# Decode through two layers: cache tiles of 8 MB in two places, fixed places for the weights

## The chip, the cores and the metric

The kernel runs on one core of a Trainium2 chip. The metric is the time of one execution on the device in microseconds (us), the median of several runs. The core has a matrix engine (PE, with its weight loads shown as PEld), a vector engine (DVE), a scalar engine (ACT), GpSimd (POOL), and a sync engine (SP) that here issues nearly all loads. Sixteen DMA engines move the data between main memory and the on-chip buffer, whose 128 partitions hold all tiles.

## What is computed

One decode step of a small transformer, for 8 sequences of one token each, through an attention block and an MLP, and then once more through the same two blocks with the same weights and the same caches. All data are float32.

```
x = A_x                                        # (8, 1, 1024)
repeat twice:
    h = layernorm(x)
    q = (h @ wq) -> 8 x 32 heads x 128         # wq 1024 x 4096
    scores = q . k_cache * 128**-0.5           # caches 8 x 4 heads x 4096 x 128
    o = softmax(scores) . v_cache              # 8 query heads share a cache head
    x = x + o @ wo                             # wo 4096 x 1024
    h = layernorm(x)
    x = x + gelu(h @ w1 + b1) @ w2 + b2        # w1 1024 x 3584, w2 3584 x 1024
```

Keys and values are 8 MB each for one sequence ("batch" below), 128 MB in all, and are read in both layers. wq and wo have 16 MB each, w1 and w2 14 MB each.

## The kernel before

**One stream of loads.** All caches and weights are cut into tiles, and `stream` lists them in the order in which they are wanted. They go into one arena of 52 units of 0.5 MB (1024 float32 columns in each partition). `pump` (L207) takes the first tile of the stream, looks among the starting units that its entry allows for a run of free units (`Arena.take`, L57: the run that has been free longest, then the lowest), issues its DMA on SP and goes on; if there is no free run it returns. `release` (L219) frees a tile's units once the matmuls that read it have been written into the program, and pumps again. So the order of DMAs on SP is fixed when the program is built, each DMA waits on the chip until the last reader of the bytes that it overwrites is done, and a DMA that waits holds up all behind it. The waits follow the bytes, not the tiles: a load over half an old tile waits for that half's readers alone.

**Layer 0.** wq's first half (`q0`, unit 0, 8 MB) goes to units 0 to 15 and stays there for layer 1 (`kept`, as eight parts). wq's second half goes to 32 to 47. Its last 2048 columns ahead of the last `KEEP` ones are copied to PSUM, and the last `KEEP` to `spare` (`park`, L466), so that layer 1 needn't load them again. The caches of batches 0 to 7 go through units 16 to 47 in tiles of 4 MB, four places (`KV_AT`); only the last values have two tiles of 2 MB (`HALF_AT`). Units 48 to 51 are for the scores and the probabilities (`OWN`). The keys of the last batch stay in 16 to 31, since layer 1 takes the batches in reverse order. The weights wo, w1 and w2 then run through units 32 to 51 in tiles of mostly 2 MB, at any start that is a multiple of the tile (`ring`); the rows of w2 are taken second half first, and the first half is kept for layer 1 in units 32 to 45 (L522). Then follows what layer 1 needs of wq's second half: three tiles of 1 MB at 46, 48, 50 and three at 0, 2, 4, where `q0`'s kept parts lie until layer 1 has multiplied them.

**Layer 1.** The caches use units 0 to 31 in four places of 4 MB; wo, w1 and the second half of w2 then run through the same units in tiles of 4, 3, 2, 1 and 0.5 MB (`deep`).

**Attention for one batch** (`plan`, L426): eight key pieces of 1 MB, each four matmuls of 32 x 512 columns (`scores`, L350); the scaled copy with its maximum on DVE (L355), `probs` (exp on ACT, L371), `turn` (transposes, L381), and eight value pieces (`values`, L400), two for each of the four cache heads. After each cache head DVE sums four strips (L403, L405), `heads` multiplies them by a selector on PE (L412) and DVE scales the result (L413).

**Products with weights.** `expand` (L234) makes q and the hidden layer in two units u = 0, 1 of columns; when a unit is done its row is scaled on DVE, and its finishing step (`query_unit`, or `hidden_unit` with bias and gelu) is put in `pending`, to be written by the next `flush`, after the next tile's matmuls. `project` (L301) multiplies by wo and w2, one "kt" of 128 rows at a time: four matmuls of 256 columns, each counted twice in the profile (as are all float32 matmuls), so 8 passes for a kt. The bias b2 enters through `add_b2` after 16 kt. In layer 1, w2's kept half (14 kt, six tiles) comes first, then the streamed half.

Every load but the small first one (x and biases, on ACT) is issued by L214; the result is stored by L550.

Of the kernel before, what the change touches and what calls it, by code (L numbers as in the profile page):

```python
# [8 lines left out]
F32 = mybir.dt.float32  # L9
# [17 lines left out]
T = CH // P  # L27
NR = NH * HKV
# [6 lines left out]
SCW = W // 2  # L35
N_UNIT = 52
OWN = 48
RING = 32
R_AT = (46, 48, 50)
KV_AT = (16, 24, 32, 40), (0, 8, 16, 24)  # L40
HALF_AT = (32, 36, 40, 44), ()
QW = 40
Q_AT = (0, (B + 1) * QW - 32, (B + 1) * QW - 8, 32)
KEEP = SCW + CH
DMA_SCRATCH = 1024


class Arena:
# [49 lines left out]
def decode_layers(ctx: ExitStack, tc: tile.TileContext, x, kc, vc, wq, wo, w1, w2, out):  # L98
# [6 lines left out]
    ps_o = ctx.enter_context(tc.tile_pool(name="ps_o", bufs=2, space=PSUM))  # L105
# [19 lines left out]
    x_row, b1T, b2T = xb[:, 0:Q4], xb[:, Q4:Q4 + NFT], xb[:, Q4 + NFT:]  # L125
# [3 lines left out]
    oT, xnT = oxT[:, 0:HQ * B + PAD], oxT[:, HQ * B:]  # L129
# [7 lines left out]
    hT = oT  # L137
# [20 lines left out]
    def flush():  # L158
        while pending:
            pending.pop(0)()  # L160
# [10 lines left out]
    def row_sums():  # L171
        return by_turns("r")
# [31 lines left out]
    stream = []  # L204
# [18 lines left out]
        slot.free()  # L223
        pump()

    def tiles(name):
        i = 0
        while (name, i) in held:
            yield held.pop((name, i))
            i += 1  # L230
        if (*name, "end") in held:
            yield held.pop((*name, "end"))

    def expand(name, unit, rs, finish, hooks={}, last=None):  # L234
        for u in range(2):
            acc = ps_o.tile([P, CH], F32, tag="o", name="acc")
            at = 0
            begun = set()
            end = NT * unit
            starts = [P * sum((unit // P - e + 3) // 4 for e in range(j)) for j in range(5)]  # L240
            for i, slot in enumerate(tiles((name, u))):
                c = 0
                while c < slot.cols and at < end:
                    kt, a = divmod(at, unit)
                    n = min(unit - a, slot.cols - c)
                    for j in range(4):
                        d0, d1 = max(a, starts[j]), min(a + n, starts[j + 1])
                        if d0 < d1:
                            nc.tensor.matmul(acc[32 * j:32 * j + 32, d0 - starts[j]:d1 - starts[j]],  # L249
                                             xnT[:, kt * B:kt * B + 32], slot.ap[:, c + d0 - a:c + d1 - a],  # L250
                                             start=(j not in begun), stop=(kt == NT - 1 and d1 == starts[j + 1]))
# [46 lines left out]
        if u == 1 and st["layer"] == 0:  # L298
            nc.gpsimd.memset(qz[:, 0:2 * nt * B], 0.0)

    def project(name, ks, lhs, out_row, resid, rsum, hooks={}):  # L301
        y = ps_o.tile([P, CH], F32, tag="o", name="y")
        n = 0
        for i, slot in enumerate(tiles(name)):
            for c in range(0, slot.cols, D):
                kt = ks[n]
                for j in range(4):
                    nc.tensor.matmul(y[32 * j:32 * j + 32, 0:Q4], lhs[:, kt * B:kt * B + 32],  # L308
                                     slot.ap[:, c + j * Q4:c + (j + 1) * Q4],
                                     start=(n == 0), stop=(n == len(ks) - 1))  # L310
                n += 1
                if n in hooks:
                    hooks[n]()
                if name[0] == "p" and n == 2 * NT:
                    add_b2(y)
                if n == NR:
                    flush()
            release(slot)
            flush()
        assert n == len(ks)  # L320
        nc.vector.scalar_tensor_tensor(out_row, y[:, 0:Q4], 1.0, resid, op0=ALU.mult, op1=ALU.add, accum_out=rsum)  # L321
# [169 lines left out]
    def caches(layer, order, skip, cuts):  # L491

        for b in order:
            for a, where, dram in (("k", k_at, kc), ("v", v_at, vc)):
                r = 0
                for m in cuts.get((a, b), (4, 4)):
                    lane = [(a, *where(b, e)) for e in range(r, r + m)]
                    if lane[0] not in skip:
                        for e, key in enumerate(lane):
                            pieces[layer, key] = ((layer, lane[0]), e)  # L500
                        yield ((layer, lane[0]), 2 * m, dram[b][:, r * W:(r + m) * W], (KV_AT if m == 4 else HALF_AT)[layer], ())
                    r += m

    rsum = row_sums()
# [1 line left out]

    kept = {("k", *k_at(B - 1, r)) for r in range(NR)}
    orders = [list(range(B)), list(range(B))[::-1]]
    ring = lambda k, i: range(RING, N_UNIT - k + 1, k)
    deep = lambda k, i: range(0, RING - k + 1, 8 if k > 4 else k)  # L510
    fixed = lambda *at: lambda k, i: (at[i],)
    last_q = [2] * 5 + [2.5]
    early = NFT // 2

    weights(("q0", 0), wq[0], [16], fixed(0), kept=lambda i: [(("q1", 0), e) for e in range(8)])
    weights(("q0", 1), wq[1], [16], fixed(RING))
    stream.extend(caches(0, orders[0], (), {("v", B - 1): (4, 2, 2)}))
    weights("o0", wo[0], [4] * 8, ring)
    for u in range(2):
        weights(("i0", u), w1[u], [4, 4, 4, 2], ring)  # L520
    weights("p0", w2[0], [4, 4, 4, 2], ring, early * D)
    weights("p0", w2[0], [4, 4, 2, 2, 1, 1], fixed(32, 36, 40, 42, 44, 45), 0, 4, lambda i: [("p1", i)])  # L522
    weights(("q1", 1), wq[1], last_q, fixed(*R_AT, 0, 2, 4))
    stream.extend(caches(1, orders[1], kept, {}))
    weights("o1", wo[0], [8] * 4, deep)
    for u in range(2):
        weights(("i1", u), w1[u], [8, 6], deep)
    weights("p1", w2[0], [4, 4, 2, 2, 1, 1], deep, early * D, 6)
    pump()
    for layer in range(2):  # L530
        st["layer"] = layer
        rs = layernorm(x_row, rsum)
        if layer == 0:
            expand("q0", W, rs, query_unit, last=park)
        else:
            held["q1", 1, "end"] = Kept(spare)
# [3 lines left out]
        project(f"o{layer}", range(HQ), oT, x_row, x_row, rsum, {4: last})  # L540
        rs = layernorm(x_row, rsum)
        expand(f"i{layer}", F // 2, rs, hidden_unit)
        rsum = row_sums()
        ks = list(range(NFT))
        if layer == 0:
            flush()
            ks = ks[early:] + ks[:early]
        project(f"p{layer}", ks, hT, x_row, x_row, rsum)

    nc.sync.dma_start(out=out, in_=x_row)  # L550

# [56 lines left out]
```

## Time and profile before

| | |
|---|---|
| median of 3 runs | 871.49 us (871.17 to 872.06) |
| the profiled execution | 872.42 us, span 870.6 us |
| TensorE clock granted, mean | 0.806 |
| bytes read from main memory | 368.46 MB |
| loads issued by L214 | 111 |

The span reaches from the first to the last instruction of the program; 1.8 us of the profiled execution lie around it. Times in windows and timelines are us from the span's start. In a timeline row stand start, duration, engine, line, operation, output<-inputs, shape and count, and in brackets the idle time of the engine ahead of the group and what ended it. A window row has start:end and length, the busy time of each engine with its instructions in brackets, and at its end the granted clock, the DMA engines' busy share and GB/s. The slices in the page are 1/40 of the span, 21.8 us.

### The profile page before, as it was taken

The page shows a single profiled execution, that of the slowest core. Times are in us where ns is not written, and L with a number is a line of the kernel's source. Part 1 is how long each engine was busy: PE and PEld are TensorE (multiplying, and loading weights), DVE is VectorE, ACT ScalarE, POOL GpSimd, SP SyncE. Part 2 cuts the span into 40 slices and gives each one's busy share as a digit, 9 for nine tenths or more (in the row PEclk, how much of TensorE's full clock was granted, in tenths as well). Part 3 has the DMA queues.
Part 4 walks back from the last instruction along what each step waited for, and adds up shares of the span by engine and source line. Part 5 has one row for each costly group of instructions (what it writes and reads, how often), then busy time and mean ns, then how long its engine had stood idle before and what let it go on. Part 6 is the DMA issues. An engine that isn't in the chain of part 4 may idle for free.

```text
span 870.6 us, 9005 instructions
## 1 busy us (share of the span) xinstructions
PE 554.2 (64%) x3988; PEld 191.5 (22%) x3988; DVE 182.6 (21%) x588; ACT 48.7 (6%) x76; POOL 1.7 (0%) x11
## 2 busy tenths in 40 slices
PE   0477566756756555756768767665667667565667
PEld 0122121221212122222223222121222212122324
DVE  0013131313223131300111232131313222130002
ACT  0010000000000000000001100000000000000000
POOL 0000000000000000000000000000000000000000
PEclk9887886788688878888779987678768778777889
DMA  9999999999999999999999999999999999999997
GB/s 391 434 434 433 432 434 428 425 434 431 427 431 431 433 434 425 388 429 430 424 409 411 436 431 431 434 433 432 429 431 428 432 431 428 431 433 430 429 425 291
DMA packets 16312, 369.17 MB, mean 424 GB/s; under 512 B 1809, under 2 KB 2065, under 8 KB 2577
## 3 DMA queue, kind: packets, MB, share of 16 engines
q1 hardware_dynamic: 16128, 368.45, 98.9%
q8 instruction: 31, 0.51, 0.2%
q10 hardware_dynamic: 144, 0.15, 0.0%
q14 instruction: 9, 0.07, 0.0%
HBM read 368.46 MB, written 0.13 MB: 423 GB/s over the span
## 4 chain that ended last, share of the span: by engine, by line
DMA 75%; PE 20%; DVE 2%; issue 1%; ACT 1%; another core or an unknown queue 1%; SPq 0%; ACTq 0%; DVEq 0%
DMA arena<-in_k_dram 53%; PE sps L350 11%; DMA arena<-in_w_dram 10%; DMA arena<-in_wo_dram 7%; DMA arena<-in_wq_dram 6%; PE acc L249 3%; PE y L308 3%; PE o_ps L400 1%; PE sps L381 0%; PE sps L274 0%; DVE scr L405 0%; SPq L214 0%; ACT arena L371 0%; DVE arena L355 0%
## 5 line engine op out<-in xcount | busy, mean ns | idle before, releaser
L350 PE MATMUL sps<-arena,qz 128*32 128x512 f32 x1024 | 170.9, 827 | 103.4 <-DMA arena<-in_k_dram 102.1
L400 PE MATMUL o_ps<-arena 128*32 128x512 f32 x1024 | 156.1, 738 | 1.0 <-DMA arena<-in_v_dram 1.0
L308 PE MATMUL y<-arena,oxT 128*32 128x256 f32 x960 | 75.9, 469 | 42.0 <-DMA arena<-in_wo_dram 30.9
L350 PEld LDWEIGHTS sps<-arena,qz 128*32 128x32 f32 x1024 | 42.2, 145 | 228.9 <-issue 182.4
L249 PE MATMUL acc<-arena,oxT 128*32 128x512 f32 (+3 forms) x510 | 71.1, 652 | 31.9 <-DMA arena<-in_w_dram 20.8
L355 DVE TENSOR_SCALAR_CACHE_REDUCE arena<-sps 128x512 f32<-128x512 f32 x32 | 22.1, 692 | 238.2 <-PE sps L350 238.2
L405 DVE SCALAR_TENSOR_TENSOR scr<-o_ps,bits,scr 128x128 f32<-128x128 f32 x192 | 67.3, 351 | 6.8
L381 PE MATMUL sps<-ident,arena 128*128 128x128 f32 x128 | 29.8, 376 | 37.4 <-DVE oxT L413 22.7
L308 PEld LDWEIGHTS y<-arena,oxT 128*32 128x32 f32 x960 | 34.5, 131 | 81.0 <-DMA arena<-in_wo_dram 33.2
L371 ACT ACTIVATE arena<-arena,bits 128x1024 f32<-128x1024 f32 x16 | 18.4, 1147 | 538.1 <-DVE scr L368 507.1
L412 PE MATMUL sps<-bits,scr 128*128 128x8 f32 x128 | 25.1, 269 | 36.4 <-DVE scr L405 31.0
L400 PEld LDWEIGHTS o_ps<-arena 128*32 128x32 f32 x1024 | 31.6, 129 | 64.6 <-issue 59.8
L403 DVE TENSOR_SCALAR scr<-o_ps,bits 128x128 f32<-128x128 f32 x64 | 22.5, 351 | 92.8 <-PE o_ps L400 92.8
L412 PEld LDWEIGHTS sps<-bits,scr 128*128 128x128 f32 x128 | 19.3, 190 | 88.5 <-DVE scr L405 79.6
L249 PEld LDWEIGHTS acc<-arena,oxT 128*32 128x32 f32 x510 | 21.5, 121 | 71.9 <-issue 34.1
L381 PEld LDWEIGHTS sps<-ident,arena 128*128 128x128 f32 x128 | 19.2, 187 | 43.4 <-ACT arena L371 27.7
L364 PE MATMUL sps<-scr,bits 128*128 128x128 f32 x32 | 7.8, 326 | 21.3 <-DVE scr L360 21.3
L387 DVE COPY arena<-sps 128x512 f32<-128x512 f32 x16 | 11.1, 692 | 43.0 <-PE sps L381 43.0
L181 PE MATMUL sps<-ident,xb 128*128 128x128 f32 x16 | 4.0, 338 | 25.1 <-DMA xb<-in_x_dram 23.4
L321 DVE SCALAR_TENSOR_TENSOR xb<-y,xb 128x256 f32<-128x256 f32 x4 | 1.7, 425 | 81.3 <-PE y L308 81.3
L389 PE MATMUL sps<-scr,bits 128*128 128x32 f32 x32 | 10.2, 412 | 12.5 <-DVE arena L387 12.5
L413 DVE TENSOR_TENSOR oxT<-sps,scr 128x8 f32<-128x8 f32 x64 | 11.0, 171 | 29.8 <-PE sps L412 29.8
(67 smaller groups left out, 128.9 us busy)
## 6 DMA issues: line engine op xcount, KB each, us to landing
arena<-in_v_dram SPq DMA_DIRECT2D x31, 4096.0 KB, 29.0
arena<-in_k_dram SPq DMA_DIRECT2D x30, 4096.0 KB, 33.4
arena<-in_w_dram SPq DMA_DIRECT2D x13, 2048.0 KB, 20.0
arena<-in_wo_dram SPq DMA_DIRECT2D x8, 2048.0 KB, 16.4
arena<-in_wo_dram SPq DMA_DIRECT2D x4, 4096.0 KB, 33.3
arena<-in_w_dram SPq DMA_DIRECT2D x2, 4096.0 KB, 32.0
arena<-in_w_dram SPq DMA_DIRECT2D x7, 1024.0 KB, 21.2
arena<-in_w_dram SPq DMA_DIRECT2D x2, 3072.0 KB, 31.1
```

Source lines behind the costliest of these rows:

```text
L249: nc.tensor.matmul(acc[32 * j:32 * j + 32, d0 - starts[j]:d1 - starts[j]], xnT[:, kt * B:kt * B + 32], slot.ap[:, c + d0 - a:c + d1 - a], ...
L308: nc.tensor.matmul(y[32 * j:32 * j + 32, 0:Q4], lhs[:, kt * B:kt * B + 32], slot.ap[:, c + j * Q4:c + (j + 1) * Q4], start=(n == 0), stop= ...
L350: nc.tensor.matmul(ps[32 * g:32 * g + 32, :], qz[:, c:c + 32], kt[:, g * CH:(g + 1) * CH], start=(j == 0), stop=(j == HKV - 1))
L355: nc.vector.tensor_scalar(st["row", b].ap[:, half * CH:(half + 1) * CH], ps, SCALE, None, op0=ALU.mult, op1=ALU.max, accum_out=st["mx", b] ...
L371: nc.scalar.activation(row, row, AF.Exp, bias=bias, scale=1.0, accum_out=ls)
L381: nc.tensor.transpose(pp[:, t * P:(t + 1) * P], row[:, c:c + P], ident)
L387: nc.vector.tensor_copy(dst, src)
L400: nc.tensor.matmul(o[32 * g:32 * g + 32, :], s[:, g], v[:, g * CH:(g + 1) * CH], start=(half == 0), stop=(half == NH - 1))
L403: nc.vector.tensor_scalar(r, o[:, 0:P], sel_t[:, 0:1], None, op0=ALU.mult)
L405: nc.vector.scalar_tensor_tensor(r, o[:, t * P:(t + 1) * P], sel_t[:, t:t + 1], r, op0=ALU.mult, op1=ALU.add)
L412: nc.tensor.matmul(po[:, 0:REP], r_s[j % 2], sel_h, start=True, stop=True)
L413: nc.vector.tensor_tensor(oT_v[:, j * REP:(j + 1) * REP, b], po[:, 0:REP], rl_s[b % 2][:, j * REP:(j + 1) * REP], ALU.mult)
```

## The change

Caches now come in tiles of 8 MB, whole keys or values of a batch, in two places: units 16 and 32 in layer 0, 0 and 16 in layer 1 (`CACHE_AT`). `CUTS` names the few that are cut: the last batch of layer 0, the first two tiles that are loaded in layer 1, and its last values. The weights of layer 0 after the attention have tiles of 3 MB for the most part, each with a place given by hand (`fixed`); in layer 1 wo comes in two tiles of 8 MB. `KEEP` grows by 3 x 128 columns, `DMA_SCRATCH` falls from 1024 to 64, and the last tile of wq shrinks to match. `project` is split: `products` multiplies a number of tiles, and in layer 1 a hook in `expand` calls it after the second tile of w1's second half, for the first two kept tiles of w2 (12 kt, with b2 after 8); `project` then goes on from there.

```diff
-KV_AT = (16, 24, 32, 40), (0, 8, 16, 24)
-HALF_AT = (32, 36, 40, 44), ()
+CACHE_AT = (16, 48), (0, 32)
+CUTS = {(0, "k", B - 1): (4, 2, 2), (0, "v", B - 1): (2, 2, 2, 2), (1, "v", B - 1): (4, 4), (1, "k", B - 2): (4, 4), (1, "v", 0): (4, 4)}
-KEEP = SCW + CH
-DMA_SCRATCH = 1024
+KEEP = SCW + CH + 3 * P
+DMA_SCRATCH = 64
...
-    def project(name, ks, lhs, out_row, resid, rsum, hooks={}):
-        y = ps_o.tile([P, CH], F32, tag="o", name="y")
-        n = 0
-        for i, slot in enumerate(tiles(name)):
+    def products(y, name, ks, lhs, n, i0, m, hooks={}):
+        for i, slot in zip(range(m), tiles(name, i0)):
...
+    def project(name, ks, lhs, out_row, resid, rsum, hooks={}, begun=None):
+        y, n, i = begun or (ps_o.tile([P, CH], F32, tag="o", name="y"), 0, 0)
+        n = products(y, name, ks, lhs, n, i, len(ks), hooks)
...
-                for m in cuts.get((a, b), (4, 4)):
+                for m in CUTS.get((layer, a, b), (NR,)):
...
-                        yield ((layer, lane[0]), 2 * m, dram[b][:, r * W:(r + m) * W], (KV_AT if m == 4 else HALF_AT)[layer], ())
+                        at = range(CACHE_AT[layer][0], CACHE_AT[layer][1], 2 * m)
+                        yield ((layer, lane[0]), 2 * m, dram[b][:, r * W:(r + m) * W], at, ())
...
-    weights("o0", wo[0], [4] * 8, ring)
-    for u in range(2):
-        weights(("i0", u), w1[u], [4, 4, 4, 2], ring)
-    weights("p0", w2[0], [4, 4, 4, 2], ring, early * D)
-    weights("p0", w2[0], [4, 4, 2, 2, 1, 1], fixed(32, 36, 40, 42, 44, 45), 0, 4, lambda i: [("p1", i)])
+    weights("o0", wo[0], [4, 4, 6, 6, 6, 6], fixed(32, 36, 40, 46, 32, 40))
+    weights(("i0", 0), w1[0], [6, 6, 2], fixed(46, 32, 38))
+    weights(("i0", 1), w1[1], [6, 6, 2], fixed(40, 46, 38))
+    weights("p0", w2[0], [6, 6, 2], fixed(32, 40, 38), early * D)
+    weights("p0", w2[0], [6, 6, 1, 1], fixed(32, 40, 38, 39), 0, 3, lambda i: [("p1", i)])
...
-    weights("o1", wo[0], [8] * 4, deep)
-    for u in range(2):
-        weights(("i1", u), w1[u], [8, 6], deep)
-    weights("p1", w2[0], [4, 4, 2, 2, 1, 1], deep, early * D, 6)
+    weights("o1", wo[0], [16, 16], fixed(16, 0))
+    weights(("i1", 0), w1[0], [8, 6], fixed(16, 24))
+    weights(("i1", 1), w1[1], [4, 4, 4, 2], fixed(0, 4, 8, 12))
+    weights("p1", w2[0], [6, 4, 2, 1, 1], fixed(16, 24, 28, 22, 23), early * D, 4)
...
+            begun = []
+
+            def begin():
+                y = ps_o.tile([P, CH], F32, tag="o", name="y")
+                begun.extend((y, products(y, "p1", ks, hT, 0, 0, 2, {NT: add_b2}), 2))
+
+            expand("i1", F // 2, rs, hidden_unit, {(1, 1): begin})
+            rsum = row_sums()
+            project("p1", ks, hT, x_row, x_row, rsum, begun=begun)
```

More of the change, by code (lines that the diff above doesn't have):

```diff
@@ L224, in release, with tiles @@
         pump()
-    def tiles(name):
-        i = 0
+    def tiles(name, i=0):
         while (name, i) in held:
@@ L312, in project @@
                 if n in hooks:
-                    hooks[n]()
-                if name[0] == "p" and n == 2 * NT:
-                    add_b2(y)
+                    hooks[n](y)
                 if n == NR:
@@ L319, in project @@
             flush()
+        return n
+    def project(name, ks, lhs, out_row, resid, rsum, hooks={}, begun=None):
+        y, n, i = begun or (ps_o.tile([P, CH], F32, tag="o", name="y"), 0, 0)
+        n = products(y, name, ks, lhs, n, i, len(ks), hooks)
         assert n == len(ks)
@@ L489, in weights, with caches @@
             at += n
-    def caches(layer, order, skip, cuts):
+    def caches(layer, order, skip):
         for b in order:
@@ L508, in decode_layers, with fixed @@
     orders = [list(range(B)), list(range(B))[::-1]]
[L509 to L512, printed above, removed]
     early = NFT // 2
+    def fixed(*at):
+        return lambda k, i: (at[i],)
     weights(("q0", 0), wq[0], [16], fixed(0), kept=lambda i: [(("q1", 0), e) for e in range(8)])
     weights(("q0", 1), wq[1], [16], fixed(RING))
-    stream.extend(caches(0, orders[0], (), {("v", B - 1): (4, 2, 2)}))
-    weights("o0", wo[0], [4] * 8, ring)
-    for u in range(2):
-        weights(("i0", u), w1[u], [4, 4, 4, 2], ring)
-    weights("p0", w2[0], [4, 4, 4, 2], ring, early * D)
-    weights("p0", w2[0], [4, 4, 2, 2, 1, 1], fixed(32, 36, 40, 42, 44, 45), 0, 4, lambda i: [("p1", i)])
-    weights(("q1", 1), wq[1], last_q, fixed(*R_AT, 0, 2, 4))
-    stream.extend(caches(1, orders[1], kept, {}))
-    weights("o1", wo[0], [8] * 4, deep)
-    for u in range(2):
-        weights(("i1", u), w1[u], [8, 6], deep)
-    weights("p1", w2[0], [4, 4, 2, 2, 1, 1], deep, early * D, 6)
+    stream.extend(caches(0, orders[0], ()))
+    weights("o0", wo[0], [4, 4, 6, 6, 6, 6], fixed(32, 36, 40, 46, 32, 40))
[3 more added lines that the diff above has]
+    weights("p0", w2[0], [6, 6, 1, 1], fixed(32, 40, 38, 39), 0, 3, lambda i: [("p1", i)])
+    last_q = (2 * NR * SCW - W - KEEP) / SCW
+    last_q = [2] * 5 + [last_q - 10]
+    weights(("q1", 1), wq[1], last_q, fixed(*R_AT, 0, 2, 4))
+    stream.extend(caches(1, orders[1], kept))
+    weights("o1", wo[0], [16, 16], fixed(16, 0))
+    weights(("i1", 0), w1[0], [8, 6], fixed(16, 24))
+    weights(("i1", 1), w1[1], [4, 4, 4, 2], fixed(0, 4, 8, 12))
+    weights("p1", w2[0], [6, 4, 2, 1, 1], fixed(16, 24, 28, 22, 23), early * D, 4)
     pump()
@@ L539, in decode_layers @@
         rsum = row_sums()
-        project(f"o{layer}", range(HQ), oT, x_row, x_row, rsum, {4: last})
+        project(f"o{layer}", range(HQ), oT, x_row, x_row, rsum, {4: lambda y: last()})
         rs = layernorm(x_row, rsum)
-        expand(f"i{layer}", F // 2, rs, hidden_unit)
-        rsum = row_sums()
         ks = list(range(NFT))
         if layer == 0:
+            expand("i0", F // 2, rs, hidden_unit)
             flush()
-            ks = ks[early:] + ks[:early]
-        project(f"p{layer}", ks, hT, x_row, x_row, rsum)
+            rsum = row_sums()
+            project("p0", ks[early:] + ks[:early], hT, x_row, x_row, rsum, {2 * NT: add_b2})
+        else:
+            begun = []
[3 more added lines that the diff above has]
+            expand("i1", F // 2, rs, hidden_unit, {(1, 1): begin})
+            rsum = row_sums()
+            project("p1", ks, hT, x_row, x_row, rsum, begun=begun)
     nc.sync.dma_start(out=out, in_=x_row)
```

## The prediction

> **What bounds the kernel now.** I read the page first, then the windows, then the timelines of PE and SP.
>
> ```profile
> PE 554.2 (64%) x3988; PEld 191.5 (22%) x3988; DVE 182.6 (21%) x588; ACT 48.7 (6%) x76; POOL 1.7 (0%) x11
> GB/s 391 434 434 433 432 434 428 425 434 431 427 431 431 433 434 425 388 429 430 424 409 411 436 431 431 434 433 432 429 431 428 432 431 428 431 433 430 429 425 291
> q1 hardware_dynamic: 16128, 368.45, 98.9%
> q8 instruction: 31, 0.51, 0.2%
> DMA 75%; PE 20%; DVE 2%; issue 1%; ACT 1%; another core or an unknown queue 1%; SPq 0%; ACTq 0%; DVEq 0%
> ```
>
> One queue moves 368.45 MB, its packets fill 98.9% of the sixteen DMA engines' time, and no other engine is busy for more than 64%. In most slices the rate is 431 to 434 GB/s. At 434 the bytes alone are 368.45/0.434 = 849 us of the 870.6, so the change can win only bytes, overhead per DMA, or the 21.6 us that lie outside the full rate. These windows show where that is.
>
> ```profile
> 22.00:44.00 22.00, 10.16 (x92) 4.37 (x96) 1.87 (x5) 2.41 (x5) 0.00 (x0) 0.84 1.00 434
> 350.00:356.00 6.00, 5.73 (x33) 1.40 (x36) 1.93 (x6) 0.00 (x0) 0.00 (x0) 0.63 0.77 284
> 450.00:454.00 4.00, 1.13 (x16) 0.50 (x16) 0.00 (x0) 0.00 (x0) 0.00 (x0) 0.93 0.90 336
> 470.00:474.00 4.00, 4.00 (x48) 1.26 (x48) 0.16 (x1) 1.78 (x4) 0.00 (x0) 1.00 0.99 369
> 490.00:840.00 350.00, 224.26 (x1496) 76.84 (x1496) 80.07 (x261) 16.75 (x28) 0.00 (x0) 0.78 1.00 431
> 862.00:867.00 5.00, 5.00 (x98) 3.03 (x92) 0.00 (x0) 0.00 (x0) 0.00 (x0) 1.00 0.36 143
> ```
>
> The last two columns are the DMA engines' busy share and GB/s. Against 434 the hole at 350 costs 6 x 150/434 = 2.07 us, that at 450 costs 4 x 98/434 = 0.90, that at 470 costs 4 x 65/434 = 0.60. The last row says something else: 0.64 x 5 = 3.2 us of a mean engine are idle while the latest of the sixteen still works, so the engines drift some 3 us apart, and a tile has landed only when the latest has.
>
> **The steady batch.** These PE rows are one batch of layer 0: keys in two halves, values, next keys.
>
> ```profile
> 92.22 5.02 PE L350 MATMUL sps<-arena,qz 128*32 128x512 f32 x32 [3.33 <-DMA arena<-in_k_dram]
> 102.02 5.25 PE L350 MATMUL sps<-arena,qz 128*32 128x512 f32 x32 [4.77 <-DMA arena<-in_k_dram]
> 115.26 4.59 PE L400 MATMUL o_ps<-arena 128*32 128x512 f32 x24
> 126.89 1.07 PE L400 MATMUL o_ps<-arena 128*32 128x512 f32 x8
> 131.07 6.08 PE L350 MATMUL sps<-arena,qz 128*32 128x512 f32 x32 [3.11 <-DMA arena<-in_k_dram]
> out_dram<-xb SPq DMA_DIRECT2D x1, 128.0 KB, 1.7
> ```
>
> 131.07 - 92.22 = 38.85 us for four 4 MB tiles: 9.71 each. Half the keys take PE 5.0 to 6.1 us, from the end of the keys to the first value matmul 115.26 - 107.27 = 8.0 us pass (softmax and transposes), the values take 126.89 + 1.07 - 115.26 = 12.7 us. From issue to first byte I take 1.7 us, the whole of a 128 KB store, so an upper figure.
>
> With two places of 8 MB a place is reloaded only when all of it is read. Let the keys land at L. They are read by L + 10.6 (12.3 at worst, two halves of 6.1); the values land at L + 19.4 and start then, since L + 10.6 + 8.0 is earlier; they are read by L + 32.2. The keys' place can be filling at L + 10.6 + 1.7 = L + 12.3, needed at L + 19.4: **7 us spare**. The values' place can be filling at L + 33.9, and is needed when the next keys have landed, L + 38.7: **4.8 us spare** for the latest engine. The 3.2 us of drift fit in. So I cost the loss of four places at nothing; the cover is that 4.8 us.
>
> **The change, part by part.**
>
> *Bytes.* KEEP grows by 384 columns: 128 x 384 x 4 = 0.197 MB of wq are no longer read twice, 0.197/0.434 = **0.45 us**. The cost is a longer copy on ACT beside q0, ahead of the first value load, which is wanted only at 63; nothing. What the smaller DMA scratch does no row shows; every DMA on the page's list is issued by SP or ACT and keeps its form, so I put nothing.
>
> *Fewer DMAs.* Counting the stream in both files, 111 loads become 79: caches 63 to 39, wo 12 to 8, w1 12 to 12, w2 16 to 12, wq 8 in both. What one costs is read from tiles of other sizes.
>
> ```profile
> 376.94 1.93 PE L308 MATMUL y<-arena,oxT 128*32 128x256 f32 x32 [1.55 <-DMA arena<-in_wo_dram]
> 381.84 3.57 PE L308 MATMUL y<-arena,oxT 128*32 128x256 f32 x32 [2.96 <-DMA arena<-in_wo_dram]
> 465.41 0.64 PE L308 MATMUL y<-arena,oxT 128*32 128x256 f32 x8 [0.18 <-DMA arena<-in_w_dram]
> 466.68 0.64 PE L308 MATMUL y<-arena,oxT 128*32 128x256 f32 x8 [0.64 <-DMA arena<-in_w_dram]
> 1.18 42.44 DMA arena<-in_wq_dram
> ```
>
> 2 MB come every 4.90 us, 4 MB every 9.71, 0.5 MB every 1.27: two halves cost 2 x 4.90 - 9.71 = 0.09 us more than the whole. 8 MB at 434 GB/s are 19.33, against 2 x 9.71 = 19.42, again 0.09. The two 8 MB tiles of wq took 42.4 us together with start-up, the bias load and some code, and that is the bound from the bad side (rival C). Between 0 and 0.09 I take 0.06: 32 x 0.06 = **1.9 us**. The Trainium skill, DMA: Bandwidth & Descriptors, Anatomy of one DMA, fits 2.0 us of fixed cost for each DMA (fitted for DMAs from GpSimd, so its use for SP's queue is my stretch). In series that would be 64 us for 32 DMAs and no such sum fits these rows: here queued DMAs cover it (rival D).
>
> *The hole at 350.* The first wo tile goes where the first values of the last batch lay and is issued when head group 0 is read.
>
> ```profile
> 336.68 5.34 PE L350 MATMUL sps<-arena,qz 128*32 128x512 f32 x32 [4.35 <-DMA arena<-in_k_dram]
> 349.94 5.01 PE L400 MATMUL o_ps<-arena 128*32 128x512 f32 x24
> 353.64 22.15 SPq L214 DMA_DIRECT2D arena<-in_wo_dram  x8
> ```
>
> The last keys land at 336.5, so the values end at 336.5 + 9.7 + 4.9 + 4.9 = 356.0; wo can flow only from 353.64 + 1.7 = 355.3, and engines that are 3 us ahead stand idle. In the new kernel the last keys come in three pieces. The stream is 0.8 us earlier by then (13 joined pairs at 0.06), so the last piece lands at 335.9. Its 16 passes take 2.7 us, but the values of batch 6 end at 316.4 + 0.1 + 12.7 = 329.2, after which the three pieces run 5.4 + 2.7 + 2.7: keys read at 340.0, values from 348.0, head group 0 read at 351.7, wo flows from 353.4, while the values' last tile lands at 355.3. Engines over 1.9 us ahead still wait a little (about 0.35 in the mean). Gain 2.07 - 0.35 = **1.7 us**; bounds 0.6 (if the 1.3 us on the latest engine were code, see B) and 2.07.
>
> *The weights between.* Places of 3 MB are refilled when a tile 6 kt long is read, and each of wo, w1 has over 4 us spare: a 6-kt tile takes PE 4.5 us at most and 7.3 us to load, with two others ahead of it. The 450 hole came of four small tiles whose places waited for one tile; now the first kept w2 tile needs the first late tile (landing near 436, read by 440) and is wanted at 446. It goes: **0.9 us**; bounds 0 and 0.9.
>
> *A new wait at 470.* These rows show what ends w2 and starts q1.
>
> ```profile
> 445.75 4.48 PE L308 MATMUL y<-arena,oxT 128*32 128x256 f32 x48 [2.97 <-DMA arena<-in_w_dram]
> 469.35 1.07 PE L249 MATMUL acc<-arena,oxT 128*32 128x512 f32 x8
> 453.56 19.92 SPq L214 DMA_DIRECT2D arena<-in_wq_dram  x6
> 476.63 7.78 SPq L214 DMA_DIRECT2D arena<-in_v_dram  x2
> ```
>
> Three wq tiles (2.47 us each, 7.4 us) need no wait; the fourth waits for PE to read the first kept q1 tile (470.4 before, 3.8 us after the last w2 tile landed). Now the last 3 MB of w2 lands only 2.5 us ahead of the end, and its 6 kt take 4.5 us after a wait, then two single kt: PE finishes 2.8 us after the last landing instead of 0.7. So the fourth wq flows at 3.8 + 2.1 + 1.7 = 7.6 us after that landing and is needed at 7.4: 0.2 us for the latest engine, and those ahead lose their lead. Behind it on SP stand two wq tiles and all caches of layer 1. The first cache tile then waits for eight kept tiles as before, about 1 us ahead of need. Mean loss between 0.2 and 2, of which 0.6 was there: I take **-0.9 us**.
>
> *The end.* Multiplying the first 12 kept kt of w2 inside w1 moves 96 passes off the last stretch.
>
> ```profile
> 792.67 41.90 SPq L214 DMA_DIRECT2D arena<-in_w_dram  x10
> arena<-in_w_dram SPq DMA_DIRECT2D x1, 512.0 KB, 32.4
> 855.07 5.39 PE L308 MATMUL y<-arena,oxT 128*32 128x256 f32 x96
> 861.92 5.55 PE L308 MATMUL y<-arena,oxT 128*32 128x256 f32 x94
> 867.52 0.42 DVE L321 SCALAR_TENSOR_TENSOR xb<-y,xb 128x256 f32<-128x256 f32 x1 [5.91 <-PE y L308]
> ```
>
> The last tile is issued at 834.25 and lands 32.4 us later, 866.65; PE is done 0.87 later, against 0.7 after layer 0's last tile. In the new order 14 kt (6.3 us at 0.45) follow gelu, which ends about 8 us before the last landing: the tail stays, +0.1 to -1.0. I take **0**. The gain of that edit is that two 8 MB wo tiles, which let PE start w1 some 5 us later, cost nothing.
>
> **Sum.** 0.45 + 1.9 + 1.7 + 0.9 - 0.9 = 4.05 us. The profiled execution took 872.42 us, 1.8 around its span of 870.6; it becomes 868.4, and the median of the runs, 871.49, becomes **867.4**. Best ends: 0.45 + 2.9 + 2.07 + 0.9 + 0.4 + 0.1 = 6.8, so 864.7; one code load (0.51 MB/31 = 16 KB, 0.6 us on one engine) that misses the latest engine makes it 864.0. Worst: 0.45 + 0 + 0.6 + 0 - 1.4 - 1.0 = -1.35, so 872.8.
>
> **The rivals.**
>
> A, slower: the values' place comes free too late. Place: the 8 MB value load of every batch, behind L400. It decides from 4.8 us more on the chain keys, softmax, values; each us beyond is paid in each of about 12 batches with whole tiles. Against: the rows above. For: PE will stand idle 6 us at a stretch instead of 3 to 5, and a PE that has been idle is slower (granted clock 0.63 at 350, 0.58 in the window below; 1.00 in the last). Keys wholly at half speed would take 21 us, not 10.6: values start at L + 29, end at L + 41.7, 4.7 us late, x 12 = 56 us. Only part slow, 6 us on the chain: 1.2 x 12 = 14 us, 882 us. Chance 8%.
>
> ```profile
> 446.00:450.00 4.00, 4.00 (x48) 1.78 (x40) 0.00 (x0) 0.00 (x0) 0.00 (x0) 0.58 1.00 424
> ```
>
> The Trainium skill, TensorE: Matmul & The Clock Gate, HAM oscillation, speaks against the change here: gaps in PE work over about 3.4 us drop the clock to half. The rows agree in kind: 6.08 against 5.02 us for the same half after gaps.
>
> B, little gained: the change doesn't close the holes, because they are code loads, or the 470 wait takes what they gave. What stays is bytes and half of the overhead, 0.45 + 0.95 = 1.4 us: 870.1. For: the DMA share at 470 was 0.99 with only 369 GB/s, so not all of a hole is waiting. Chance 13%.
>
> C, slower: 8 MB tiles load worse, 20.5 us rather than 19.4 (42.44 less about 1.5 of start, halved). 28 such tiles more, 1.1 each: 31 us, 902 us. Against: 434 GB/s in the window 22 to 44, which moves nothing but wq. Chance 3%.
>
> D, 2 us saved for each DMA: 64 us, 807 us. Against: 368.1 MB in that time would be over 455 GB/s, and no slice has over 436. Chance 1%.
>
> **The numbers.** 0.2% is 1.7 us, about what a measurement of this kernel can tell from no change: faster is under 869.7, slower over 873.2. The forecast has 75%, nearly all of it faster; B 13%, three parts in four within 0.2%. Faster 0.75 + 0.01 + 0.01 = 0.77, same 0.11, slower 0.12. Range 864.0 to 872.0: the best end, and B with most of the worst end; A, C and D stay out.
>
> **What would show it.** Steady batches 0.1 to 0.3 us shorter than 38.85; value loads issued 4 to 5 us before the keys ahead of them land; 420 GB/s and more at 350 and 450; a hole at 470 of 1 to 2 us; last landing some 4 us earlier, then 0.7 to 1.0 us to the last DVE step. Slices under 425 GB/s all through the attention would make the prediction wrong by A or C: SP waiting for L400 beyond the landing is A, 20.5 us a tile without such a wait is C.

## The result and the profile after

The changed kernel takes **868.02 us** (median of 5 runs, 867.59 to 868.36) beside 872.06 us for the kernel before (871.17 to 873.39, 5 runs): ratio 0.9951, 95% interval 0.9936 to 0.9965. The profiled execution took 868.16 us with a span of 866.4 (before: 872.42 and 870.6). Run again beside the experiments it took 868.49 us (867.49 to 869.17), ratio 0.9953 (0.9941 to 0.9966).

From the page of the kernel after: totals, rate in slices of 21.7 us, the load queue, and the chain that ended last.

```profile
PE 526.5 (61%) x3998; PEld 188.6 (22%) x3998; DVE 182.6 (21%) x588; ACT 49.0 (6%) x76; POOL 1.7 (0%) x11
GB/s 393 437 436 433 436 430 433 433 433 433 436 434 433 436 405 430 430 429 428 428 404 404 440 444 433 430 430 433 433 436 433 436 433 430 415 446 430 412 428 294
q1 hardware_dynamic: 11520, 368.25, 99.0%
DMA 71%; PE 24%; DVE 3%; another core or an unknown queue 1%; issue 1%; ACT 0%; SPq 0%; ACTq 0%; DVEq 0%
```

The bytes are 0.20 MB fewer, the packets 4608 fewer. The slice at 350 (the 17th) has 430 GB/s where it had 388; the two slices from 433 to 477 have 404, so nothing was won there in the mean of the engines. The windows say the same (last columns: DMA share, GB/s). Slices and windows count a packet whole where it starts, and packets of an 8 MB tile have 64 KB and take 2.42 us, so a share can come out above 1.00 and a rate some per cent off: the 405 in the 15th slice is 431 when its packets are counted by the time that they lie in it.

```profile
350.00:356.00 6.00, 5.22 (x44) 1.61 (x36) 2.96 (x10) 0.00 (x0) 0.00 (x0) 0.88 1.01 431
446.00:450.00 4.00, 2.56 (x40) 1.14 (x32) 0.00 (x0) 0.00 (x0) 0.00 (x0) 0.87 0.98 410
450.00:454.00 4.00, 1.00 (x18) 0.64 (x20) 0.00 (x0) 0.00 (x0) 0.00 (x0) 0.98 0.98 356
454.00:460.00 6.00, 5.21 (x44) 1.84 (x38) 0.69 (x1) 0.00 (x0) 0.00 (x0) 0.50 0.92 390
466.00:470.00 4.00, 3.85 (x49) 1.19 (x52) 0.73 (x3) 2.06 (x4) 0.00 (x0) 1.00 0.97 383
490.00:840.00 350.00, 211.52 (x1518) 73.93 (x1514) 81.86 (x268) 18.34 (x30) 0.00 (x0) 0.79 1.00 432
```

The hole at 350 is closed (284 to 431). The one at 450 is still there, 356 GB/s, but at a share of 0.98: most engines are in packets that move less, and few are idle. In 490 to 840 the rate is 432 instead of 431.

The steady batch, from PE's timeline: both halves of the keys, the first and last value matmuls, and the next keys; then the value load in SP's timeline.

```profile
101.77 5.57 PE L350 MATMUL sps<-arena,qz 128*32 128x512 f32 x32 [7.00 <-DMA arena<-in_k_dram]
108.17 3.64 PE L350 MATMUL sps<-arena,qz 128*32 128x512 f32 x32 [0.83 <-DVE arena L355]
121.13 5.27 PE L400 MATMUL o_ps<-arena 128*32 128x512 f32 x24 [0.79 <-DMA arena<-in_v_dram]
132.75 1.07 PE L400 MATMUL o_ps<-arena 128*32 128x512 f32 x8
140.47 1.93 PE L350 MATMUL sps<-arena,qz 128*32 128x512 f32 x8 [6.66 <-DMA arena<-in_k_dram]
```

```profile
133.88 0.33 SPq L214 DMA_DIRECT2D arena<-in_v_dram  x1
```

A batch takes 140.47 - 101.77 = 38.70 us, where it took 38.85. PE takes 12.7 us for the values, as before, and 10.0 for the keys. The value load is issued at 133.88, 6.55 us ahead of the landing of the keys in front of it: less the 1.7 us to its first byte, 4.85 us are spare, as reckoned.

Where the 4.1 us arose is best seen in the landings of single loads (issue plus time to landing in the list of issues, us):

| landing of | before | after | gain so far |
|---|---|---|---|
| layer 0's last values | 356.03 | 355.23 | 0.80 |
| its last wo tile | 396.69 | 394.25 | 2.44 |
| its last w2 tile | 466.64 | 463.20 | 3.44 |
| the last wq tile | 482.11 | 479.51 | 2.60 |
| layer 1's last values | 776.08 | 771.36 | 4.72 |
| the last load | 866.64 | 862.52 | 4.12 |

### The profile page after: what moved, and what is told of

It reads as the page before. It is cut to its first block, busy times and chain, and to the rows that moved or that the text cites. A ratio compares the mean times of both kernels' runs of the same rounds, so it can differ in the third digit from the quotient of the medians.

```text
span 866.4 us, 8937 instructions
## 1 busy us (share of the span) xinstructions
PE 526.5 (61%) x3998; PEld 188.6 (22%) x3998; DVE 182.6 (21%) x588; ACT 49.0 (6%) x76; POOL 1.7 (0%) x11
## 4 chain that ended last, share of the span: by engine, by line
DMA 71%; PE 24%; DVE 3%; another core or an unknown queue 1%; issue 1%; ACT 0%; SPq 0%; ACTq 0%; DVEq 0%
DMA arena<-in_k_dram 47%; PE sps L350 16%; DMA arena<-in_w_dram 11%; DMA arena<-in_wo_dram 7%; DMA arena<-in_wq_dram 6%; PE y L305 3%; PE acc L248 2%; PE o_ps L400 2%; DVE arena L355 1%; DVE scr L405 1%; PE sps L381 0%; ACT arena L371 0%; PE sps L273 0%; PE sps L412 0%
## 5 line engine op out<-in xcount | busy, mean ns | idle before, releaser
L350 PE MATMUL sps<-arena,qz 128*32 128x512 f32 x1024 | 146.5, 721 | 109.2 <-DMA arena<-in_k_dram 96.8
L400 PE MATMUL o_ps<-arena 128*32 128x512 f32 x1024 | 154.3, 731 | 16.6 <-DMA arena<-in_v_dram 16.6
L350 PEld LDWEIGHTS sps<-arena,qz 128*32 128x32 f32 x1024 | 35.3, 129 | 216.9 <-issue 101.9
L248 PE MATMUL acc<-arena,oxT 128*32 128x512 f32 (+3 forms) x518 | 65.5, 607 | 25.4 <-DMA arena<-in_w_dram 14.2
L305 PEld LDWEIGHTS y<-arena,oxT 128*32 128x32 f32 x960 | 36.9, 134 | 86.9 <-issue 34.4
L381 PE MATMUL sps<-ident,arena 128*128 128x128 f32 x128 | 32.0, 397 | 37.5 <-DVE oxT L413 22.7
L248 PEld LDWEIGHTS acc<-arena,oxT 128*32 128x32 f32 x518 | 21.7, 117 | 60.2 <-issue 28.7
```

Source lines behind the costliest of these rows:

```text
L350: nc.tensor.matmul(ps[32 * g:32 * g + 32, :], qz[:, c:c + 32], kt[:, g * CH:(g + 1) * CH], start=(j == 0), stop=(j == HKV - 1))
L381: nc.tensor.transpose(pp[:, t * P:(t + 1) * P], row[:, c:c + P], ident)
L400: nc.tensor.matmul(o[32 * g:32 * g + 32, :], s[:, g], v[:, g * CH:(g + 1) * CH], start=(half == 0), stop=(half == NH - 1))
```

## The experiments

Times are medians; the changed kernel is at 868.0 (first five runs) and 868.5 (run again), the kernel before at 872.0 to 872.6.

**The changed kernel again.**

> The changed kernel beside the experiments. The sum's theory: bytes 0.45 us, 32 fewer DMAs 1.9, the hole at 350 1.7, the hole at 450 and the wait at 470 together 0, so about 4 us less than the kernel before, 868.0 again, with the last load landing near 862.5. A rival: the gain belongs to the pair of executions that were compared, and less than 2 us of it is left.

868.49 us, last load landing at 861.8. The gain is there again.

**Whole caches in 4 MB tiles.**

```diff
-                for m in CUTS.get((layer, a, b), (NR,)):
+                for m in CUTS.get((layer, a, b), (4, 4)):
```

> Only the tile size of the caches goes back: whole keys and values in two tiles of 4 MB each, places as they fall free, the small tiles at the last batch of layer 0 and all else as in the changed kernel. 105 loads instead of 79. Theory (0.06 us for each DMA): 26 x 0.06 = 1.6 us more than the changed kernel, 869.6, evenly along the attention, 38.85 us a batch instead of 38.7. Rival (the size of a tile costs nothing, the gain is in the holes alone): 868.0.

869.68 us (869.43 to 870.62), 1.2 to 1.7 more than the changed kernel, and evenly. Its PE timeline, the second key halves of two neighbouring batches:

```profile
102.23 5.34 PE L350 MATMUL sps<-arena,qz 128*32 128x512 f32 x32 [4.11 <-DMA arena<-in_k_dram]
141.09 2.79 PE L350 MATMUL sps<-arena,qz 128*32 128x512 f32 x12 [4.77 <-DMA arena<-in_k_dram]
```

141.09 - 102.23 = 38.86 us a batch instead of 38.70: 0.08 for each of two DMAs saved. By the landings it is 2 x 9.71 - 19.36 = 0.06. The theory holds.

**8 MB caches in the kernel before**, that is the same part from the other side.

```diff
-                for m in cuts.get((a, b), (4, 4)):
+                for m in CUTS.get((layer, a, b), (NR,)):
...
-KV_AT = (16, 24, 32, 40), (0, 8, 16, 24)
-HALF_AT = (32, 36, 40, 44), ()
+CACHE_AT = (16, 48), (0, 32)
+CUTS = {(0, "k", B - 1): (4, 4), (0, "v", B - 1): (4, 2, 2), (1, "v", B - 1): (4, 4), (1, "k", B - 2): (4, 4), (1, "v", 0): (4, 4)}
...
```

> The kernel before with one part of the change: whole keys and values of 8 MB in two places, the last batch of layer 0 cut as before (4+4, 4+2+2), weights, kept columns and w2 as before. 85 loads instead of 111. Theory: 26 x 0.06 = 1.6 us less than the kernel before, 870.2; the holes at 350 and 450 stay. Rival A of the prediction (places come free too late): longer than before.

870.67 us (868.53 to 873.69, a wide spread), ratio 0.9983 (0.9970 to 0.9996): 1.4 us less by the medians, beside the 1.6 expected; the interval reaches from 0.3 to 2.6. Rival A isn't seen.

**The last batch's cuts as before.**

```diff
-CUTS = {(0, "k", B - 1): (4, 2, 2), (0, "v", B - 1): (2, 2, 2, 2),
+CUTS = {(0, "k", B - 1): (4, 4), (0, "v", B - 1): (4, 2, 2),
```

> Only the cuts of layer 0's last batch go back: keys in two tiles of 4 MB, values in 4, 2 and 2 MB. The last keys' passes after landing grow from 2 to 5.3 us, so the first wo tile is issued near 352.5 and flows near 354.2, while the last values land near 355.2. Theory (the mean engine pays): the hole at 350 returns, 280 to 330 GB/s in 350 to 356, and the time is 1.7 us longer, 869.6. Rival (only the engine that lands last counts, and it isn't late at 354.2): the hole is seen in the window, but the time stays within 0.4 us of the changed kernel's.

868.38 us, ratio 0.9951 (0.9939 to 0.9964): no loss beside the 868.49 of the changed kernel run again. Its window has the hole, as deep as before the change:

```profile
350.00:356.00 6.00, 5.39 (x42) 1.41 (x34) 1.80 (x6) 0.00 (x0) 0.00 (x0) 0.76 0.74 281
```

The last wo tile does land 1.1 us later (395.3 instead of 394.25): the third wo tile, of 3 MB, takes 8.51 us behind the second, where such tiles take 7.31. Of this only 0.4 is left at the first value tile of layer 1 (489.6 and 489.2), since the fourth wq tile comes 2.48 us behind the third here and 3.75 in the changed kernel. The last load lands at 862.71, 0.2 us later than in the first profile of the changed kernel and 0.9 later than in that of its repetition. So a hole in the rate isn't yet a loss of time: here it cost its own stage 1.1 us, which a wait behind it took up.

**The last batch in whole tiles.**

```diff
-CUTS = {(0, "k", B - 1): (4, 2, 2), (0, "v", B - 1): (2, 2, 2, 2), (1, "v", B - 1): (4, 4),
+CUTS = {(1, "v", B - 1): (4, 4),
```

> Layer 0's last batch has whole tiles of 8 MB, too; nothing else changes. The last keys land at 335.4 and take 10 us, the values land near 354.7 and start then, the first head group is read near 358.3 and wo flows near 360.0. Theory: even the latest engine is idle for 5.2 us; less 0.3 for 5 fewer DMAs this gives about 4.9 us more than the changed kernel, 873, that is the whole gain of the change. Rival (the queue makes it good in the weights between): under 2 us.

874.82 us (874.09 to 875.96): 6.3 to 6.8 more. The windows and SP's first wo issue:

```profile
350.00:356.00 6.00, 3.76 (x18) 2.05 (x22) 1.05 (x2) 0.60 (x1) 0.00 (x0) 0.54 0.24 101
356.00:362.00 6.00, 6.00 (x38) 1.51 (x30) 1.82 (x6) 0.00 (x0) 0.00 (x0) 0.61 0.44 147
```

```profile
358.49 15.10 SPq L214 DMA_DIRECT2D arena<-in_wo_dram  x5
```

wo is issued at 358.5 while the values landed at 354.7: here the latest engine waits, too, and this is paid in full and more (the last wo tile lands at 401.15, 6.9 us later). The small tiles are what makes 8 MB places bearable at the end of the attention.

**Layer 0's weights as before.**

```diff
-    weights("o0", wo[0], [4, 4, 6, 6, 6, 6], fixed(32, 36, 40, 46, 32, 40))
+    weights("o0", wo[0], [4] * 8, ring)
...
-    weights("p0", w2[0], [6, 6, 1, 1], fixed(32, 40, 38, 39), 0, 3, lambda i: [("p1", i)])
+    weights("p0", w2[0], [4, 4, 2, 2, 1, 1], fixed(32, 36, 40, 42, 44, 45), 0, 4, lambda i: [("p1", i)])
...
```

> Only layer 0's weights between the attentions go back to tiles of 2, 1 and 0.5 MB at the places of the kernel before (86 loads instead of 79; the first 12 kept kt of w2 then lie in four tiles). Theory: 7 x 0.06 = 0.4 us for the DMAs, 0.9 for the hole at 450, and 0.9 back, since the last w2 tiles are small again and the fourth wq tile no longer comes late: 0.4 us more, 868.4. Rival 1 (the hole at 450 was places, the wait at 470 is free): 1.3 us more. Rival 2 (the hole at 450 is no wait for places, the wait at 470 costs): 0.5 us less.

867.89 us (867.66 to 868.31), ratio 0.9954 (0.9940 to 0.9967): 0.1 to 0.6 less than the changed kernel, which can't be told from nothing. The dip in the rate is there again, some 3 us earlier and as deep (336 GB/s), but the late landing behind it is not, though tiles, places and order are those of the kernel before. A window and PE's and SP's timelines:

```profile
446.00:450.00 4.00, 1.23 (x20) 0.42 (x16) 0.00 (x0) 0.00 (x0) 0.00 (x0) 1.00 0.88 336
```

```profile
444.22 1.94 PE L305 MATMUL y<-arena,oxT 128*32 128x256 f32 x32 [1.26 <-DMA arena<-in_w_dram]
446.71 1.07 PE L305 MATMUL y<-arena,oxT 128*32 128x256 f32 x16 [0.55 <-DMA arena<-in_w_dram]
```

```profile
447.84 3.16 SPq L214 DMA_DIRECT2D arena<-in_w_dram  x5
```

The same six kt that took one stretch of 4.48 us before (quoted in the prediction, at 445.75, granted clock 0.58) take 1.94 + 1.07 here at full clock. Before, the loads behind them were issued at 450.3, 2.8 us ahead of the landing of the load in front, and the first landed 6.1 us after that one; here they are issued at 447.84, 3.7 us ahead, and that step is 4.9 us, the rule for 2 MB. Of the 2.5 us by which the issue is earlier, 1.5 are those by which the tiles themselves land earlier (446.66 and 448.19 for the last of the six kt); PE's clock makes the other 0.9.

**Both as before**, cuts and weights together, the rest of the change staying.

> Layer 0's weights and the cuts of its last batch go back together (each alone left the time where it was: 867.9 and 868.4); the 8 MB caches, the kept columns, the early product and layer 1's weights stay. 84 loads. If the two replace each other (the hole at 350 or the one at 450 is paid once, as long as one of the two old parts stands, the other's loss is taken up by a later wait), the 2 us that no single part accounts for come back here: 870 to 870.5, near the 870.7 of the kernel before with 8 MB caches. If neither matters, so that the rest lies in the kept columns and in layer 1's end: 867.9 to 868.6.

870.49 us (867.79 to 872.35), ratio 0.9976 (0.9964 to 0.9988): 2.0 to 2.5 more than the changed kernel, where each part alone cost nothing. From its PE timeline and its window at 350:

```profile
445.93 4.48 PE L305 MATMUL y<-arena,oxT 128*32 128x256 f32 x48 [2.97 <-DMA arena<-in_w_dram]
```

```profile
350.00:356.00 6.00, 5.64 (x32) 1.63 (x36) 1.76 (x5) 0.00 (x0) 0.00 (x0) 0.61 0.58 208
```

The slow stretch of six kt is back, 4.48 us, and with it the late loads (issued from 450.5, the first one 6.9 us behind its forerunner). The wo stage takes 41.8 us from the last values to the last wo tile, against 39.0 in the changed kernel and 40.2 with the old cuts alone. So by the medians the two parts replace each other; by what mechanism is not shown. The profiled execution is the longest of the twelve (872.35), and its first wo tile is issued 1.27 us later than with the old cuts alone (354.02 and 352.75), mostly because PE took 6.33 us for the last half of the keys and not 5.34. Up to there the two programs are the same, so that part is a difference between executions and not the work of the second edit. Whether the short executions, down to 867.8, have the stretch of six kt at full clock was not seen. What this kernel has beyond the kernel before with 8 MB caches (kept columns, the smaller DMA scratch, the early product, layer 1's weights) brought nothing that can be told: 870.49 beside 870.67.

**Without the early product.**

```diff
-            expand("i1", F // 2, rs, hidden_unit, {(1, 1): begin})
+            expand("i1", F // 2, rs, hidden_unit)
...
-            project("p1", ks, hT, x_row, x_row, rsum, begun=begun)
+            project("p1", ks, hT, x_row, x_row, rsum, {2 * NT: add_b2})
```

> Only the early multiplication of kept w2 is undone: all 28 kt of layer 1's w2 follow after w1. Theory: after the last w1 tile (845.3) PE has 28 kt at 0.45, 2 us of bias and 0.7 of transposes, 15.5 us, so it ends near 861, before the last tile lands at 862.5: no change, 868.0 to 868.4. Rival (the early product carries the end): PE ends behind the last landing by the 7 us that were moved, up to 5 us more.

867.87 us (867.44 to 868.07): no change. The last two groups of its PE timeline show that PE still waits for the last two tiles:

```profile
861.23 0.64 PE L305 MATMUL y<-arena,oxT 128*32 128x256 f32 x8 [0.54 <-DMA arena<-in_w_dram]
862.47 0.64 PE L305 MATMUL y<-arena,oxT 128*32 128x256 f32 x8 [0.61 <-DMA arena<-in_w_dram]
```

**Kept w2 in shrinking tiles**, meant to be better.

```diff
-    weights("p0", w2[0], [6, 6, 1, 1], fixed(32, 40, 38, 39), 0, 3, lambda i: [("p1", i)])
+    weights("p0", w2[0], [6, 4, 2, 1, 1], fixed(32, 40, 44, 38, 39), 0, 3, lambda i: [("p1", i)])
...
```

> A version meant to be better: w2's kept half is loaded as 3, 2, 1, 0.5, 0.5 MB instead of 3, 3, 0.5, 0.5, so that PE ends nearer to its last landing and the fourth wq tile is issued about 1.5 us earlier against the stream. Theory (the wait at 470 costs the latest engine about 1.3 us: 3.75 us between landings there, where 2.48 is the rule): 0.7 to 1.3 us less than the changed kernel, 867. Rival (engines ahead lose only their lead, which nobody needs): no change, plus 0.06 for one more DMA.

867.40 us (867.26 to 869.09), ratio 0.9952 (0.9937 to 0.9966): 0.6 to 1.1 less by the medians, but not told apart by the runs. The fourth wq tile now comes 2.50 us after the third and not 3.75. But the first value tile of layer 1 takes 11.09 us behind the last wq tile, where it took 9.71, and lands at 489.02 instead of 489.22: in this execution the loss moved and did not go. The window still has its dip:

```profile
466.00:470.00 4.00, 4.00 (x48) 1.13 (x44) 0.16 (x1) 2.04 (x4) 0.00 (x0) 1.00 0.96 365
```

**More work for PE in each batch**, 12 matmuls in the changed kernel, and 28 in both kernels.

```diff
             if j == HKV - 1:
+                pd = small_ps("pt")
+                for e in range(12):
+                    g = e % NG
+                    nc.tensor.matmul(pd[32 * g:32 * g + 32, :], s[:, g], v[:, g * CH:(g + 1) * CH], start=True, stop=True)
                 release(st.pop(("S", b)))
```

> The changed kernel with 12 more matmuls of 32 x 512 at the end of each batch's values, on the last value piece, their result unused: about 2.7 us more for PE in each batch, ahead of the release of the values' place. Theory (4.8 us are spare there): no change, within 0.5 us of 868.0. Rival (the spare time is already used up by engines that run ahead): 12 batches pay part of it, 5 us or more.

> The same with 28 more matmuls, about 6.4 us for PE in each batch. Theory: 6.4 - 4.8 = 1.6 us beyond the spare time, paid in each of 12 batches, and about 1 at the second wo tile: 15 to 20 us more than the changed kernel, 883 to 888, with a batch of 40.2 us instead of 38.7. Rival (PE has 6.5 us idle in a batch, so 6.4 fit): no change.

> The kernel before, with the same 28 more matmuls in each batch. With four places of 4 MB the values' second place is wanted only some 20 us after it is read, and PE's 5.3 + 8.0 + 12.7 + 6.4 + 5.0 = 37.4 us a batch fit in 38.85. Theory: no change but up to 1 us at the ends of the attentions, 872 to 873. If instead PE's own time is what the work adds to, this kernel gets as much longer as the changed one.

With 12 matmuls: **875.10 us** (873.01 to 878.39), about 7 more, where the theory said none. With 28: **899.10 us** (898.39 to 899.98), 31 more, where it said 15 to 20. The kernel before with the same 28: 873.91 us, ratio 1.0019 (1.0009 to 1.0030), 1.5 more. So the cover of the four places is there and that of the two is much thinner than 4.8 us. In the changed kernel with 12 matmuls, PE's timeline, the load that waits for them, and two windows:

```profile
133.65 2.76 PE L411 MATMUL sps<-arena 128*32 128x512 f32 x24
140.73 5.34 PE L350 MATMUL sps<-arena,qz 128*32 128x512 f32 x32 [4.32 <-DMA arena<-in_k_dram]
```

```profile
136.47 0.33 SPq L214 DMA_DIRECT2D arena<-in_v_dram  x1
```

```profile
596.00:601.00 5.00, 1.27 (x8) 0.40 (x12) 0.00 (x0) 0.00 (x0) 0.00 (x0) 0.81 0.99 341
490.00:840.00 350.00, 223.63 (x1684) 77.33 (x1679) 80.03 (x261) 16.75 (x28) 0.00 (x0) 0.82 0.99 423
```

The 12 matmuls take 2.76 us. The load is issued 140.69 - 136.47 = 4.2 us before the keys land, so its first byte may flow 2.5 us before the latest engine needs it. Nevertheless the stretch 490 to 840 runs at 423 GB/s instead of 432, and around the changes of tile it drops to 341 (596 to 601): engines ahead of the latest have nothing to do, and the first packets after the wait move less. Counted by the time that they lie in the window, packets fill 0.93 of it and move 338 GB/s, so the idle time is the smaller part of the loss: packets of 64 KB that start between 597 and 600.5 take 2.7 to 4.0 us instead of 2.42. Not every batch pays. Of the twelve 8 MB value tiles that wait for the added work, six land within 0.25 us of the usual 19.35 behind the keys, and six land 0.6 to 2.1 us later than that, 7.6 us in sum.

## Why the prediction was right

The forecast, 867.4 in a range of 864.0 to 872.0, is 0.6 us from the result; the sum of 4.05 us stands beside 4.26 in the profiled executions (872.42 to 868.16). So close a sum is luck in part, since the last landing alone differs by 0.7 us between two executions of the changed kernel (862.52 and 861.84). Its terms fared differently.

*Bytes, 0.45.* The page has 0.20 MB less, as said. The time of it alone was not tried, nor the smaller DMA scratch; it is below what the runs tell apart.

*Fewer DMAs, 1.9 for 32.* Right in size and place. The two cache experiments give 1.2 to 1.7 us for 26 loads, 0.05 to 0.065 each. The landings agree: with the step that each size takes where nothing waits (8 MB 19.36, 4 MB 9.71, 3 MB 7.31, 2 MB 4.89, 1 MB 2.47, 0.5 MB 1.25), all loads behind the first add up to 834.7 us before and 832.3 after, 2.4 less, beside 0.45 + 1.9. The rest of the gain is in the steps that are longer than that. Rival C fell: keys and values land every 19.36 us in steady batches (38.70/2 = 19.35), below 2 x 9.71. Rival D fell with it: the 26 loads gave back 1.5 us and not 52. The Trainium skill's fixed 2.0 us for each DMA (DMA: Bandwidth & Descriptors, Anatomy of one DMA), fitted there for DMAs from GpSimd, is no cost in series on this queue, which is kept full; the measurement decides.

*The hole at 350, 1.7, and the hole at 450, 0.9.* In the table of landings the stages have these sizes: 2.44 - 0.80 = 1.64 and 3.44 - 2.44 = 1.0, of which some 0.1 and 0.3 belong to the two and five fewer DMAs there. But the steps behind them failed as separate terms. "The hole at 350 ... Gain 1.7" was read from GB/s, the mean of the engines; with the old cuts the same hole cost 1.1 us in the wo stage and nothing in the end. "The 450 hole came of four small tiles whose places waited for one tile; ... It goes" named the place of the wait, but the dip did not go (356 GB/s, so the sign "420 GB/s and more at 350 and 450" failed at 450), and the new tiles were not needed against the late landing: with the old ones PE read them at full clock and the loads came in time. Undone together the two parts cost 2.0 to 2.5 us, some 0.3 of it for five more DMAs, beside the 2.6 of the sum, so the total of the two terms was about right and the split was not.

*The wait at 470, -0.9.* From the last w2 tile to the last wq tile it takes 16.31 us after and 15.47 before, and the last wq tile is 0.45 us shorter: the loss was 1.3 in this execution, and 0.6 by the landings of the repeated run (15.63). The step behind it was off: PE ended 1.2 us after the last w2 tile and not 2.8, since its last 64 passes ran at full clock, 3.66 us:

```profile
460.71 3.66 PE L305 MATMUL y<-arena,oxT 128*32 128x256 f32 x64 [0.48 <-DMA arena<-in_w_dram]
```

The fourth wq tile was issued at 467.5 and could flow at 469.2, ahead of the third one's landing at 470.65. So the latest engine was not kept waiting, as "0.2 us for the latest engine" had it; those ahead were, and the tile landed 3.75 us after the third.

*The end, 0.* Right: the last DVE step starts 0.75 us after the last landing (863.27 and 862.52), in the range given. But "the gain of that edit is that two 8 MB wo tiles ... cost nothing" fell: without the early product those tiles cost nothing either.

```profile
863.27 0.42 DVE L321 SCALAR_TENSOR_TENSOR xb<-y,xb 128x256 f32<-128x256 f32 x1 [9.62 <-PE y L305]
```

*Rival A.* It did not happen, and the spare time was reckoned rightly, 4.85 us. The slower PE that spoke for it was small: after an idle stretch of 7.00 us the first half of the keys took 5.57 us, at a granted clock of 0.50 for its first 2.78 us and 0.79 behind them, and the second half ran at full clock, so the keys took 10.0 us and not 21. (The rows said to "agree in kind", 6.08 against 5.02 us, show no effect of a longer gap: the 6.08 stands behind the shorter one, 3.11 us against 3.33.)

But the point from which rival A decides was wrong: "It decides from 4.8 us more on the chain" is refuted by 2.76 us more, which cost 7. The step that failed is "The 3.2 us of drift fit in": they fit, but not much beside them. (The drift itself is nearer to 2.8 us, for the last load lands at 866.64 and 0.36 us of the window that it was read from lie behind that.) With the 12 matmuls 2.3 us are still spare for the latest engine, but engines that are further ahead run dry. How much of the 4.85 us is free was not measured; 4.85 less the drift, some 1.6 to 2.0, is an estimate.

That losing the lead is what costs, because code loads then hit engines that have none, is a reading, and the profiles bear on it. A code load is one of the 31 packets of 16 KB in q8, the queue of kind "instruction" on the page; it holds one of the sixteen engines for 1.07 us in the median, not the 0.6 of the prediction. Every execution without added work has one shortly after the place of the hole at 350, at 364 to 366 (370 with the last batch in whole tiles). The step between landings in which it falls is 1.2 to 1.7 us longer than usual in all five profiled executions that have the hole (before: 6.33 us instead of 4.89; old cuts: 8.51 instead of 7.31), and at most 0.3 us longer in the six without hole or added work. With 12 matmuls, though, a code load falls in the steps of five of the six late value tiles but also of three of the six others, so it alone doesn't decide, and no run moved a code load by itself.

## What to carry to other kernels

Where one full load queue sets the time, joining tiles gains some hundredths of a microsecond per DMA, and it is safe only where a place is read well before it is wanted again: count the drift between the DMA engines as used up, and test the rest by adding work: here 2.76 us of it in each batch already cost 7 us, though 4.85 were spare by the landings. A dip in GB/s shows that some engines wait; the time follows the landings of single loads, so compare these stage by stage and undo parts in pairs, since two parts may each be enough. At a change of stage cut the tiles so that the first place falls free before the latest engine needs it; there it cost 6 us not to.

## What the runs showed of the hardware

The start of a load after a wait costs more than the wait: with 12 extra matmuls the DMA engines were in packets for 0.93 of the time from 596 to 601 and moved 338 GB/s, where queued loads move 432, because the first packets of 64 KB took up to 4.0 us instead of 2.42. Code goes through the same engines: in the changed kernel each of the eleven 8 MB cache tiles with no code load in its step landed within 0.02 us of 19.36 behind the tile in front, and the longer steps, up to 20.25, all hold one. And PE's clock reaches the loads: the same 48 passes took 4.48 us at a granted clock of 0.58 and 3.0 us at full clock, which put the issue of the next loads 0.9 us later.
